# First attention of an attention and gMLP stack on one NeuronCore: no moves on ScalarE, output weights and four residual pairs loaded in the opening, pattern work on GpSimd in pieces, ring copies later

## The chip, the cores and the metric

One core of a Trainium2 chip. The time is that of one execution on the device, in microseconds (us); lower is better. Engines: TensorE (PE: matmuls; PEld: its weight loads), VectorE (DVE), ScalarE (ACT), GpSimd (POOL) and SyncE (SP). DMAs are issued by SP, ScalarE or GpSimd and run on 16 DMA engines.

## The reference

Four layers, attention, gMLP, attention, gMLP, each with a layernorm before it and a residual sum after it, on x of 2048 rows by 576 columns in bfloat16:

```
qkv = layernorm(x) @ wqkv                 # 32 heads of 18
k, v gathered at positions s, s-2, ..., s-14   # window 8, dilation 2, masked below 0
o = softmax(q k / sqrt(18)) v
x = x + o @ wo
z = gelu(layernorm(x) @ w_in); z1, z2 = halves of z
x = x + (z1 * (w_sp @ layernorm(z2) + b_sp)) @ w_out
```

The change concerns the first attention only.

## The kernel before

The order of the work in an attention layer is written by hand: inside `layer_A` every engine runs its instructions in program order (a manual schedule, L377). Even positions of the sequence stand before odd ones, so the dilated window becomes a contiguous one, and the sequence is cut into 17 query tiles (one of 128, then 120 each) with a halo of eight keys.

**Opening** (L602 to L736). SP loads x in groups, then the weights of v and of q and k, then the rest of x; one small load is ScalarE's. `build_window_rows` (L115) makes, from a few integers, the pattern that is added to the logits as 14 extra rows per head, so that positions outside the window vanish in the softmax: `part0` on VectorE and GpSimd, `part1` and `part2` on GpSimd, `part3` six transposes on TensorE and a copy by ScalarE into `win_pat`. 46 matmuls of the identity run meanwhile. Then each tile of x goes through statistics (`S_`, VectorE), the power -1/2 of the variance (`R_`, GpSimd, L646), the layernorm (`A_`, VectorE, L653) and a transpose into `xnT`: tiles 0 to 3 on TensorE (`T_pe`), tiles 4 to 15 by a DMA transpose that SP issues (`T_`, L263). The layernorm's output lies in four buffers `xn_bufs` in turn, so tile 12 waits until the transpose of tile 8 has landed, and tile 15 for that of tile 11.

`PG(d, qk, cc)` (L416) projects one group of 128 q or k columns (groups 0 to 4; group 4 holds 64) for 512 rows: five matmuls (L435), then an eviction by ScalarE or VectorE into a staging buffer `stg` (or a part of `win2a`, lent). When q and k of 1024 rows are there, up to eight heads are moved by DMAs from staging into `QK` (L457), each to its own 32 partitions. A list of engines, taken in turn, issues these moves; in the opening GpSimd, SP and ScalarE. The 40 moves of the first half are SP's 13, GpSimd's 20 and ScalarE's 7. `VW(t, hh)` (L405) projects v of a query tile into `v_ext`.

**Steps.** After the opening come four query tiles of v, six projections (L833; the first two of them need tiles 8 to 11 of `xnT`), and the logits of half a query tile, `L_mm(0)` (L472); then a loop of 34 steps, two per query tile. Step s issues the logits of s + 1, their exponential (ScalarE, L481), the product with v (`PV`, L495), VectorE's division (L501, L503), and what a table holds for that step: remaining projections in steps 0 to 11, v from step 12 on, and the output projection `WO` (L556) from step 13 on, with its residual sum (L559), store and next layernorm (GpSimd, L256). The logits of a tile need the moves of its heads: those of the first half of the heads groups 0 to 2, the others groups 2 to 4; from query tile 8 on they need the second half of the sequence too.

`PV` leaves o in one of four `o_bufs`. SP transposes it by DMA into the ring `oT` (L510), or, where the tile does not start at a multiple of 16, into one of two `o_slot` (L514), and VectorE copies it from there into the ring later (`O_CP`, L523). The step of that copy is `min(2t + 6, s)` for tile t, where s is the step before the output projection that needs it (L790): step 10 for tile 2, 14 for tile 4, 18 for tile 6, 22 for tile 8. `XO` (L541) loads the residual rows of two tiles: those of tiles 0 to 11 in steps 0 to 2. `load_wo` loads the output weights in step 4 (L824).

**Queues and waits.** The DMAs that SP and ScalarE issue share eight completion semaphores in turn, in program order; those of GpSimd have eight others. An issue waits until the DMA that had its semaphore before has landed, so that eight are in flight at most, and an engine that waits so does nothing else. SP issues transposes, moves and loads from one list, in order. PSUM holds a ring of tiles that TensorE fills in turn; a tile that is not evicted holds TensorE up.

Of the kernel before, what the change touches and what calls it, by code (L numbers as in the profile page):

```python
# [10 lines left out]
ALU = mybir.AluOpType  # L11
# [7 lines left out]
P = 128  # L19
# [44 lines left out]
class K:  # L64
# [50 lines left out]
    def build_window_rows(self, c, Wb):  # L115
# [38 lines left out]
            for xb in self.xn_bufs:  # L154
                e.memset(xb[:, D:640], 0.0)

        def part2():
            e = nc.gpsimd
            par = vf[:, 4, 3:4]
            e.tensor_scalar(out=hh[:, 1, :], in0=hh[:, 0, :], scalar1=0.0, scalar2=WB, op0=ALU.is_ge, op1=ALU.mult)  # L160
            e.tensor_scalar(out=W[:, 0, :, 0:8], in0=hh[:, 1:2, :].to_broadcast([P, 12, 8]), scalar1=-half, scalar2=par,
                            op0=ALU.add, op1=ALU.mult)
            e.tensor_scalar(out=hh[:, 2, :], in0=hh[:, 0, :], scalar1=-2.0, scalar2=-1.0, op0=ALU.is_equal, op1=ALU.mult)
            e.tensor_scalar(out=hh[:, 3, :], in0=hh[:, 0, :], scalar1=14.0, scalar2=None, op0=ALU.is_equal)
            e.tensor_tensor(out=hh[:, 2, :], in0=hh[:, 2, :], in1=hh[:, 3, :], op=ALU.add)
# [4 lines left out]
            e.tensor_tensor(out=uu[:], in0=vf[:, 0:4, 0], in1=vf[:, 0:4, 1], op=ALU.add)  # L170
            e.tensor_scalar(out=W[:, 1, :, 8:12], in0=uu[:, None, :].to_broadcast([P, 12, 4]), scalar1=0.5, scalar2=None,
                            op0=ALU.mult)
            e.memset(W[:, 1, 8:12, 8:9], 0.0)
            e.memset(W[:, 1, 8:12, 9:12], 1.0)
            e.memset(W[:, 0, 8:12, 11:12], 1.5 * WB)
            e.memset(W[:, 0, 8:12, 13:14], -3.5 * WB)

        def part3():
            pt = self.PT_tile([P, 6, P], bf16, "pt")
            for k_ in range(6):  # L180
                nc.tensor.transpose(pt[:, k_, :], Wb[:, k_ // 3, k_ % 3].rearrange("p j q -> p (j q)"), self.ident[:])
            nc.scalar.copy(out=pat[:], in_=pt[:].rearrange("p (a b) x -> p a (b x)", a=2)[:, :, 0:2 * P + 8])
        return part0, part1, part2, part3

    def make_ident(self):
        nc = self.nc
# [108 lines left out]
        nc, R = self.nc, self.right  # L295
        nc.vector.memset(R["wv"][64:128, 4, :], 0.0)

    def zero_more(self, eng):
        eng.memset(self.right["wqk4"][64:128, :], 0.0)
        eng.memset(self.right["wo"][64:128, 4, :], 0.0)  # L300

    def load_wqk(self, eng):
# [35 lines left out]
    def layer_A(self, li):  # L338
# [263 lines left out]
        if li == 0:  # L602
# [26 lines left out]
                nc.tensor.matmul(warm[:, 0:P], lhsT=self.ident[:], rhs=self.ident[:], start=True, stop=True)  # L629
            rows[2]()  # L630
            nc.scalar.copy(out=v_ext[:, :, :, DH:DH + 1], in_=self.ones[:, None, None, :].to_broadcast([P, NT, H, 1]))
            rows[3]()
            mvs = sb.tile([P, NS, 2], f32, name="lnx_mv", tag="lnx_mv", bufs=1)
            rstds = sb.tile([P, NS], f32, name="lnx_rstd", tag="lnx_rstd", bufs=1)

# [12 lines left out]

            def A_(*tiles):
                for i in tiles:  # L650
                    xns[i] = xn = self.xn_bufs[self.xn_rr % len(self.xn_bufs)]
                    self.xn_rr += 1
                    nc.vector.tensor_scalar(out=xn[:, 0:D], in0=xts[i], scalar1=mvs[:, i, 0:1],  # L653
                                            scalar2=rstds[:, i:i + 1], op0=ALU.subtract, op1=ALU.mult)

# [42 lines left out]
            A_(3)  # L698
            T_pe(3)
# [87 lines left out]
        for t in range(NT - 2):  # L787
            s = wo_steps[q0_(t) // P][0] - 1
            r = (q0_(t) + tdim(t)[1] - 1) // P - RING
            if t < NT - 3 and not in_ring(t):  # L790
                ocps.append((min(2 * t + 6, s), t))
                assert r < 0 or wo_steps[r][1] < min(2 * t + 6, s)
# [72 lines left out]
    def layer_B(self, li):  # L865
# [286 lines left out]
        for i in range(i0, NS):  # L1152
# [3 lines left out]
            p3_finish(i, acc)  # L1156
            if next_is_A and i == 2:
                self.zero_right()
                self.zero_more(nc.vector)
            if i >= 3 and late_loads:  # L1160
                late_loads.pop(0)()
        if (NS - 2) in xns:
# [72 lines left out]
```

## Time and profile before

| | us |
|---|---|
| median of 3 runs | 1175.58 |
| lowest, highest | 1175.12, 1177.72 |
| the profiled execution | 1177.02 |
| its span in the profile | 1175.2 |
| TensorE busy | 1150.6 |
| VectorE, ScalarE, GpSimd busy | 551.2, 341.8, 271.1 |
| first attention ends, gMLP begins (first L924 matmul) | 135.32 |

The profile is of one execution. A row of the timeline gives start, length, engine, line, operation, output and inputs, shape, count (x), and in brackets how long the engine had been idle and what ended it. `SPq`, `ACTq` are issues of DMAs by these engines; an issue is over long before its DMA has landed. A row of waits gives who waited, for whom, us in total, times, and the longest. The granted clock is the share of TensorE's full speed that it was given. Busy time of TensorE is not the same as speed: at half the clock it is busy and slow.

### The profile page before, as it was taken

Reading aid. Unit: us, or ns where it says so; the run is one execution under the profiler, and the core shown is the slowest. Engines: PE = TensorE matmul, PEld = TensorE weight load, DVE = VectorE, ACT = ScalarE, POOL = GpSimd, SP = SyncE. Lnnn points to the kernel's source line nnn. Section 1 sums busy time; section 2 is a strip of 40 time slices with the busy share of each in tenths; the row PEclk is TensorE's granted clock in tenths of the full one; section 3 lists DMA queues with packets and bytes.
Section 4 is the critical chain, followed back from the end, with each engine's and each line's share of the span. In section 5 each row is a group of like instructions: output and inputs, shape, how many; then the busy total and the mean of one; then the engine's idle time right before and its main releaser. Section 6 shows DMA issues by size and latency. Waiting matters only on the chain.

```text
span 1175.2 us, 19942 instructions
## 1 busy us (share of the span) xinstructions
PE 1150.6 (98%) x8169; PEld 611.8 (52%) x8264; DVE 551.2 (47%) x1166; ACT 341.8 (29%) x500; POOL 271.1 (23%) x389
## 2 busy tenths in 40 slices
PE   8889999999999999999999999999999999999998
PEld 5447644444444444447755675444444444444677
DVE  8468888422332332334465787863323223322321
ACT  5478655211101111101147884550011110111000
POOL 4468865100000000001144686540000000000000
PEclk9899999999999999999999999999999999999999
DMA  7799889000000000049646898950000000001332
GB/s 194 124 181 226 220 187 196 23 12 12 1 12 12 12 12 1 1 139 282 172 106 109 178 284 216 196 107 1 12 12 12 12 11 2 12 1 45 110 106 73
DMA packets 183242, 106.37 MB, mean 91 GB/s; under 512 B 135165, under 2 KB 164453, under 8 KB 183151
## 3 DMA queue, kind: packets, MB, share of 16 engines
q1 hardware_dynamic: 170140, 84.66, 31.4%
q0 software_dynamic: 6384, 14.28, 4.6%
q10 hardware_dynamic: 6627, 6.17, 1.8%
q8 instruction: 64, 1.05, 0.4%
q14 instruction: 27, 0.22, 0.1%
HBM read 42.34 MB, written 21.76 MB: 55 GB/s over the span
## 4 chain that ended last, share of the span: by engine, by line
PE 93%; DMA 2%; DVE 2%; POOL 1%; issue 1%; ACT 1%; ACTq 0%; DVEq 0%; POOLq 0%; SPq 0%
PE pg L1072 42%; PE po L1121 12%; PE pz L924 6%; PE pz L1048 6%; PE pz1s L1048 6%; PE pzs L924 6%; PE pp L435 6%; PE pw L556 3%; PE pv L409 3%; PE O_ps L495 2%; PE L_ps L472 1%; DMA o_slot<-o_t 1%; DMA QK<-stg 1%; POOL ln_xn L256 1%; ACTq L78 0%
## 5 line engine op out<-in xcount | busy, mean ns | idle before, releaser
L1072 PE MATMUL pg<-Wq,Z 128*128 128x512 bf16 x2260 | 497.9, 379 | 2.5
L1072 PEld LDWEIGHTS <-Z 128*128 128x128 bf16 x2304 | 225.4, 98 | 271.9
L1076 DVE TENSOR_TENSOR g_tmp<-pg,ln_xn 128x512 f32<-128x512 f32 x144 | 99.6, 692 | 421.6 <-PE pg L1072 419.5
L1067 ACT ACTIVATE z1T<-pz 128x1024 bf16<-128x1024 f32 x36 | 34.9, 1021 | 500.2 <-PE pz L1048 500.2
L78 POOL DMA_DIRECT2D wout<-in_B_w_out_dram x4 | 4.3, 1072 | 598.8 <-PE pg L1072 598.8
L1121 PE MATMUL po<-wout,Z 128*128 128x288 bf16 x1152 | 141.4, 286 | 0.0
L481 ACT ACTIVATE P_sb<-L_ps 128x1440 bf16<-128x1440 f32 (+3 forms) x136 | 125.1, 972 | 25.4 <-PE L_ps L472 23.7
L1121 PEld LDWEIGHTS <-Z 128*128 128x128 bf16 x1152 | 112.7, 98 | 28.8
L924 PEld LDWEIGHTS <-xnT 128*128 128x128 bf16 (+1 forms) x800 | 68.3, 97 | 75.8 <-issue 10.4
L1077 DVE TENSOR_TENSOR Z<-g_tmp,z1T 128x512 bf16<-128x512 f32 x144 | 99.7, 692 | 12.2
L973 DVE BATCH_NORM_STATS2 z_st<-zp 128x6 f32<-128x512 bf16 (+1 forms) x160 | 91.2, 617 | 9.1 <-ACT zp L971 8.9
L1048 PEld LDWEIGHTS <-w 128*128 128x128 bf16 (+1 forms) x640 | 53.8, 97 | 74.0 <-issue 13.6
L435 PE MATMUL pp<-xnT,wqk_sb 128*128 128x512 bf16 x341 | 82.3, 382 | 1.3 <-issue 0.2
L1131 DVE TENSOR_TENSOR x_new<-po,xo 128x288 f32<-128x288 f32 (+1 forms) x64 | 28.8, 456 | 87.8 <-PE po L1121 83.9
L1048 PE MATMUL pz<-xnT,w 128*128 128x512 bf16 (+1 forms) x316 | 66.3, 380 | 0.2
L1048 PE MATMUL pz1s<-xnT,w 128*128 128x512 bf16 (+1 forms) x310 | 64.9, 379 | 0.9 <-issue 0.8
L256 POOL TENSOR_SCALAR ln_xn<-x_new,ln_mv,ln_rstd 128x576 bf16<-128x576 f32 x28 | 64.1, 2290 | 3.2 <-DMA xn_rows<-ln_xn 0.6
L409 PE MATMUL pv<-wv_sb,xnT 128*128 128x288 bf16 x340 | 51.9, 294 | 9.6 <-ACT v_ext L403 5.0
L924 PE MATMUL pz<-win2a,xnT 128*128 128x512 bf16 (+1 forms) x233 | 58.3, 357 | 0.9 <-DVE x_new L559 0.5
L924 PE MATMUL pzs<-win2a,xnT 128*128 128x512 bf16 (+1 forms) x235 | 58.6, 358 | 0.4 <-issue 0.3
L997 POOL TENSOR_SCALAR Z<-zp,z_mv,z_rstd 128x256 bf16<-128x256 bf16 x32 | 54.5, 1703 | 3.4
L971 ACT ACTIVATE zp<-pz 128x1024 bf16<-128x1024 f32 (+2 forms) x56 | 36.6, 720 | 63.3 <-PE pz L924 63.3
(123 smaller groups left out, 936.2 us busy)
## 6 DMA issues: line engine op xcount, KB each, us to landing
xres<-x_new SPq DMA_DIRECT2D x48, 288.0 KB
xo<-xres SPq DMA_DIRECT2D x32, 288.0 KB
wout<-in_B_w_out_dram POOLq DMA_DIRECT2D x4, 1296.0 KB, 7.9
xn_rows<-ln_xn SPq DMA_DIRECT2D x32, 160.0 KB
w<-in_B_w_in_dram SPq DMA_DIRECT2D x16, 256.0 KB
QK<-stg POOLq DMA_DIRECT2D x50, 72.0 KB, 4.5
xo<-xres SPq DMA_DIRECT2D x6, 576.0 KB
QK<-stg SPq DMA_DIRECT2D x35, 72.0 KB
```

What stands on the lines that cost most here:

```text
L256: e.tensor_scalar(out=xn[:nrows, 0:D], in0=x_t[:nrows, :], scalar1=mv[:nrows, 0:1], scalar2=rstd[:nrows, 0:1], op0=ALU.subtract, op1=ALU.mult)
L409: nc.tensor.matmul(pv[:nk, 0:288], lhsT=self.xnT[:, c, k0_(t):k0_(t) + nk], rhs=wv_sb[:, c, hh * 288:(hh + 1) * 288], start=(c == 0), stop ...
L435: nc.tensor.matmul(pp[:, :], lhsT=w, rhs=self.xnT[:, c, cc * 512:(cc + 1) * 512], start=(c == 0), stop=(c == 4))
L481: nc.scalar.activation(out=P_bufs[2 * jp + s % 2][:nk, :, :, 0:nq], in_=Lv[:nk, :, :, 0:nq], func=ACT.Exp, scale=scale)
L924: nc.tensor.matmul(out[:, o0:o0 + n], lhsT=self.xnT[r0:r1, c, r * P:(r + 1) * P], rhs=win2(c)[r0:r1, w0:w0 + n], start=start, stop=stop, t ...
L973: nc.vector.bn_stats(out=st[:, x // 512, :], in_=zp[:, x:x + min(512, w0 + n - x)])
L997: eng.tensor_scalar(out=Z[:, b0:b1, i, :], in0=zv[:, b0:b1, :], scalar1=mv[:, 0:1], scalar2=rstd[:, 0:1], op0=ALU.subtract, op1=ALU.mult)
L1048: nc.tensor.matmul(outs[a_], lhsT=w1[r0:r1, c, sub * P:(sub + 1) * P], rhs=self.xnT[r0:r1, c, q * 512:(q + 1) * 512], start=start, stop=st ...
L1072: nc.tensor.matmul(pg[:, :], lhsT=Z[:, jj, i, sub * P:(sub + 1) * P], rhs=Wq[q][:, i, :], start=(i == 0), stop=(i == NS - 1))
L1076: nc.vector.tensor_tensor(out=tmp[:], in0=pg[:, :], in1=bsp[:, qs], op=ALU.add)
L1077: nc.vector.tensor_tensor(out=uT(jj)[:, sub, qs], in0=tmp[:], in1=z1Ts[jj, sub][:, qs], op=ALU.mult)
L1121: nc.tensor.matmul(acc[hh], lhsT=u_rows(j, i), rhs=wouts[j // NJH][:, j % NJH, hh * 288:(hh + 1) * 288], start=(j == 0), stop=(j == NJ - 1))
```

## The change

- `part2` (13 operations of GpSimd) becomes `part2a` (four), `part2b`, `part2c` and `part2d`. The first still stands ahead of the power of tile 0; the others stand behind the powers of tiles 0, 1 and 2.
- The six transposes of `part3` go behind the v projection `VW(1, 1)`, and the copy, now `part4`, behind `VW(2, 0)`.
- `zero_more` becomes `zero_wqk4` and `zero_wo`; the second, and the fills of `setup_bufs`, come later on GpSimd.
- The layernorms of tiles 12 to 14 are written into `o_bufs[1]` to `[3]` instead of `xn_bufs`. Tile 15 still uses `xn_bufs`, and waits for the transpose of tile 8.
- Moves in the opening: groups 0 and 4 by GpSimd and SP in turn, groups 1 to 3 by GpSimd, SP, GpSimd. Of the 40, SP issues 16, GpSimd 24, ScalarE none.
- `load_wo` and `XO` of tiles 0 to 7 (four loads of two tiles) are issued by SP in the opening, right behind the transposes of tiles 6 and 7, instead of in steps 4, 0 and 1. `XO` of tiles 8 and 9, and of 10 and 11, goes from step 2 to steps 19 and 22.
- The ring copies of `O_CP` stand at `min(2t + 8, s)`: step 12 for tile 2, 16 for tile 4, 19 for tile 6, 23 for tile 8; the others, and all those of the second attention, stay where they were.

```diff
-        def part2():
+        def part2a():
             e.tensor_scalar(out=hh[:, 1, :], in0=hh[:, 0, :], scalar1=0.0, scalar2=WB, op0=ALU.is_ge, op1=ALU.mult)
+            e.tensor_scalar(out=hh[:, 2, :], in0=hh[:, 0, :], scalar1=-2.0, scalar2=-1.0, op0=ALU.is_equal, op1=ALU.mult)
+            e.tensor_scalar(out=hh[:, 3, :], in0=hh[:, 0, :], scalar1=14.0, scalar2=None, op0=ALU.is_equal)
+            e.tensor_tensor(out=uu[:], in0=vf[:, 0:4, 0], in1=vf[:, 0:4, 1], op=ALU.add)
+        def part2b():
...
+        def part4():
+            nc.scalar.copy(out=pat[:], in_=pts[0][:].rearrange("p (a b) x -> p a (b x)", a=2)[:, :, 0:2 * P + 8])
...
-            rows[3]()
...
             def A_(*tiles):
                 for i in tiles:
-                    xns[i] = xn = self.xn_bufs[self.xn_rr % len(self.xn_bufs)]
-                    self.xn_rr += 1
+                    if 12 <= i < 15:
+                        xn = o_bufs[i - 11][:]
+                    else:
+                        xn = self.xn_bufs[self.xn_rr % len(self.xn_bufs)]
+                        self.xn_rr += 1
+                    xns[i] = xn
...
             S_(0)
             R_(0, 1)
             S1(1)
+            rows[3]()
             A_(0)
             S2(1)
             R_(1, 1)
+            rows[4]()
             T_pe(0)
...
             S2(2)
             R_(2, 1)
+            rows[5]()
             VW(1, 0, False)
             S_(3)
             A_(2)
             R_(3, 1)
-            self.zero_more(nc.gpsimd)
-            setup_bufs(nc.gpsimd)
+            self.zero_wqk4(nc.gpsimd)
             T_pe(2)
             VW(1, 1, False)
+            rows[6]()
...
             R_(4, 2)
+            self.zero_wo(nc.gpsimd)
+            setup_bufs(nc.gpsimd)
             VW(2, 0, False)
+            rows[7]()
             VW(2, 1, False)
...
             T_(6, 7)
+            self.load_wo(nc.sync)
+            for i in range(0, 8, 2):
+                XO(i)
...
-                    PG(d, qk, cc, False, (nc.gpsimd, nc.sync, nc.gpsimd, nc.scalar, nc.gpsimd, nc.sync))
+                    PG(d, qk, cc, False, (nc.gpsimd, nc.sync) if d in (0, 4) else q2)
...
-                ocps.append((min(2 * t + 6, s), t))
+                ocps.append((min(2 * t + 8, s), t))
...
-                at(max([i // 4 if li == 0 and i < 12 else s - 7] + [wo_steps[j][1] + 1 for j in last]), XO, i)
+                if li > 0 or i >= 8:
+                    at(max([s - 7] + [wo_steps[j][1] + 1 for j in last]), XO, i)
...
-            at(4, self.load_wo, nc.sync)
```

`q2` is GpSimd, SP, GpSimd (L599).

More of the change, by code (lines that the diff above doesn't have):

```diff
@@ L155, in part1, with part2c @@
                 e.memset(xb[:, D:640], 0.0)
-        def part2():
-            e = nc.gpsimd
-            par = vf[:, 4, 3:4]
+        e = nc.gpsimd
+        par = vf[:, 4, 3:4]
+        def part2a():
             e.tensor_scalar(out=hh[:, 1, :], in0=hh[:, 0, :], scalar1=0.0, scalar2=WB, op0=ALU.is_ge, op1=ALU.mult)
+            e.tensor_scalar(out=hh[:, 2, :], in0=hh[:, 0, :], scalar1=-2.0, scalar2=-1.0, op0=ALU.is_equal, op1=ALU.mult)
+            e.tensor_scalar(out=hh[:, 3, :], in0=hh[:, 0, :], scalar1=14.0, scalar2=None, op0=ALU.is_equal)
+            e.tensor_tensor(out=uu[:], in0=vf[:, 0:4, 0], in1=vf[:, 0:4, 1], op=ALU.add)
+        def part2b():
+            e.tensor_tensor(out=hh[:, 2, :], in0=hh[:, 2, :], in1=hh[:, 3, :], op=ALU.add)
             e.tensor_scalar(out=W[:, 0, :, 0:8], in0=hh[:, 1:2, :].to_broadcast([P, 12, 8]), scalar1=-half, scalar2=par,
                             op0=ALU.add, op1=ALU.mult)
-            e.tensor_scalar(out=hh[:, 2, :], in0=hh[:, 0, :], scalar1=-2.0, scalar2=-1.0, op0=ALU.is_equal, op1=ALU.mult)
-            e.tensor_scalar(out=hh[:, 3, :], in0=hh[:, 0, :], scalar1=14.0, scalar2=None, op0=ALU.is_equal)
-            e.tensor_tensor(out=hh[:, 2, :], in0=hh[:, 2, :], in1=hh[:, 3, :], op=ALU.add)
+        def part2c():
             e.tensor_scalar(out=W[:, 1, :, 0:8], in0=hh[:, 2:3, :].to_broadcast([P, 12, 8]), scalar1=par, scalar2=None,
@@ L169, in part2, with part2d @@
                             op0=ALU.mult)
-            e.tensor_tensor(out=uu[:], in0=vf[:, 0:4, 0], in1=vf[:, 0:4, 1], op=ALU.add)
+        def part2d():
             e.tensor_scalar(out=W[:, 1, :, 8:12], in0=uu[:, None, :].to_broadcast([P, 12, 4]), scalar1=0.5, scalar2=None,
                             op0=ALU.mult)
+            e.memset(W[:, 0, 8:12, 11:12], 1.5 * WB)
+            e.memset(W[:, 0, 8:12, 13:14], -3.5 * WB)
             e.memset(W[:, 1, 8:12, 8:9], 0.0)
             e.memset(W[:, 1, 8:12, 9:12], 1.0)
-            e.memset(W[:, 0, 8:12, 11:12], 1.5 * WB)
-            e.memset(W[:, 0, 8:12, 13:14], -3.5 * WB)
+        pts = []
         def part3():
@@ L181, in part3 @@
                 nc.tensor.transpose(pt[:, k_, :], Wb[:, k_ // 3, k_ % 3].rearrange("p j q -> p (j q)"), self.ident[:])
-            nc.scalar.copy(out=pat[:], in_=pt[:].rearrange("p (a b) x -> p a (b x)", a=2)[:, :, 0:2 * P + 8])
-        return part0, part1, part2, part3
+            pts.append(pt)
+        def part4():
+            nc.scalar.copy(out=pat[:], in_=pts[0][:].rearrange("p (a b) x -> p a (b x)", a=2)[:, :, 0:2 * P + 8])
+        return part0, part1, part2a, part2b, part2c, part2d, part3, part4
     def make_ident(self):
@@ L296, in zero_right, with zero_wqk4, zero_wo @@
         nc.vector.memset(R["wv"][64:128, 4, :], 0.0)
-    def zero_more(self, eng):
+    def zero_wqk4(self, eng):
         eng.memset(self.right["wqk4"][64:128, :], 0.0)
+    def zero_wo(self, eng):
         eng.memset(self.right["wo"][64:128, 4, :], 0.0)
@@ L790, in layer_A @@
             if t < NT - 3 and not in_ring(t):
-                ocps.append((min(2 * t + 6, s), t))
-                assert r < 0 or wo_steps[r][1] < min(2 * t + 6, s)
+                ocps.append((min(2 * t + 8, s), t))
+                assert r < 0 or wo_steps[r][1] < min(2 * t + 8, s)
             else:
@@ L1158, in layer_B @@
                 self.zero_right()
-                self.zero_more(nc.vector)
+                self.zero_wqk4(nc.vector)
+                self.zero_wo(nc.vector)
             if i >= 3 and late_loads:
```

## The prediction

> **What bounds the kernel now.** I read the page first, then busy time by stretches of the first attention, then its waits, then the timeline around the two longest. In the stretches the columns are length, busy time of TensorE, its loads, VectorE, ScalarE and GpSimd, then granted clock, DMA share and GB/s.
>
> ```profile
> span 1175.2 us, 19942 instructions
> PE 1150.6 (98%) x8169; PEld 611.8 (52%) x8264; DVE 551.2 (47%) x1166; ACT 341.8 (29%) x500; POOL 271.1 (23%) x389
> ...
> 35.00:40.00 5.00, 3.45 (x27) 2.54 (x26) 0.98 (x4) 1.07 (x2) 3.86 (x7) 1.00 1.07 99
> 40.00:45.00 5.00, 1.57 (x7) 0.99 (x7) 0.90 (x2) 1.78 (x6) 2.48 (x5) 0.75 1.17 153
> 45.00:50.00 5.00, 4.78 (x18) 2.35 (x17) 1.01 (x2) 1.03 (x3) 0.14 (x1) 0.57 0.63 123
> ...
> 80.00:85.00 5.00, 0.47 (x13) 0.33 (x10) 1.19 (x4) 1.73 (x2) 2.15 (x4) 0.84 1.22 137
> 85.00:90.00 5.00, 5.00 (x63) 2.88 (x61) 2.92 (x8) 1.83 (x2) 3.06 (x6) 0.50 0.98 148
> ```
>
> TensorE is the bound of the whole, so only its holes and its slow clock are worth anything. In the first attention there are two holes, near 40 and 82 us, and after each the granted clock is about half.
>
> ```profile
> PE pv L409 <- ACT v_ext L403: 5.0, 1, 5.0
> PE pv L409 <- DVE o_t L503: 4.5, 1, 4.5
> ACT v_ext L403 <- DMA QK<-win2a: 6.1, 1, 6.1
> DVE oT L523 <- DMA o_slot<-o_t: 5.5, 1, 5.5
> ```
>
> Behind each hole stands an engine that waits for a DMA: ScalarE in the first, VectorE in the second.
>
> ```profile
> 35.23 3.23 PE L409 MATMUL pv<-wv_sb,xnT 128*128 128x288 bf16 x25
> ...
> 41.33 1.61 ACTq L78 DMA_DIRECT2D QK<-win2a  x2
> 42.98 1.61 ACT L403 CAST v_ext<-pv 128x288 bf16<-128x288 f32 x5 [6.10 <-DMA QK<-win2a]
> ...
> 45.79 0.43 DVE L653 TENSOR_SCALAR ln_xn<-x_in,lnx_mv,lnx_rstd 128x576 bf16<-128x576 bf16 x1 [1.03 <-DMA xnT<-ln_xn]
> ...
> 50.38 0.40 PE L472 MATMUL L_ps<-QK 32*128 32x128 bf16 x16
> ...
> 56.36 0.40 PE L472 MATMUL L_ps<-QK 32*128 32x128 bf16 x16
> ```
>
> First hole: TensorE ends 25 value matmuls at 38.46 and waits for ScalarE's evictions, which stand behind two moves that ScalarE issues only at 41.33. But the next projections need xnT tile 11, and the 45.79 row shows when its transpose had landed (the layernorm there reuses that buffer). So with ScalarE free, this transpose is what is late next, and most of the hole stays.
>
> ```profile
> 74.55 1.84 SPq L514 DMA_TRANSPOSE o_slot<-o_t  x1
> ...
> 79.41 0.39 PE L472 MATMUL L_ps<-QK 32*128 32x120 bf16 x16
> 79.79 2.61 SPq L78 DMA_DIRECT2D QK<-stg  x3
> ...
> 83.78 0.35 DVE L523 COPY oT<-o_slot 128x600 bf16<-128x600 bf16 x1 [5.48 <-DMA o_slot<-o_t]
> ...
> 91.87 0.39 PE L472 MATMUL L_ps<-QK 32*128 32x120 bf16 x16
> ...
> 93.93 0.39 PE L472 MATMUL L_ps<-QK 32*128 32x120 bf16 x16
> ```
>
> Second hole: the ring copy of tile 2 (step 10) holds VectorE until its transpose lands. SP issued that transpose only at 74.55, and it landed 9.2 us later. The logits of steps 13 and 16 start 12.46 us apart, where three undisturbed steps (93.93 - 91.87 = 2.06 each) take 6.2.
>
> **The change, part by part.**
>
> *Opening.*
>
> ```profile
> 3.33 0.25 POOL L160 TENSOR_SCALAR win_hh<-win_hh 128x8 f32<-128x8 f32 x1 [0.72 <-DVE win_hh L145]
> ...
> 4.82 0.81 DVE L670 BATCH_NORM_STATS2 ln_st<-x_in 128x6 f32<-128x288 bf16 x2
> 6.74 0.58 POOL L646 TENSOR_TENSOR lnx_rstd<-lnx_rstd,neg_half 128x1 f32<-128x1 f32 x1
> 6.86 0.40 PE L181 MATMUL pt<-ident,oT 128*128 128x128 bf16 x4 [0.58 <-POOL oT L176]
> 7.29 0.60 ACT L182 COPY win_pat<-pt 128x528 bf16<-128x528 bf16 x1 [2.18 <-PE pt L181]
> 7.36 0.43 DVE L653 TENSOR_SCALAR ln_xn<-x_in,lnx_mv,lnx_rstd 128x576 bf16<-128x576 bf16 x1 [1.72 <-POOL lnx_rstd L646]
> ...
> 11.70 1.02 DVE L653 TENSOR_SCALAR ln_xn<-x_in,lnx_mv,lnx_rstd 128x576 bf16<-128x576 bf16 x1
> ...
> 14.29 8.80 PE L435 MATMUL pp<-xnT,wqk_sb 128*128 128x512 bf16 x39
> ```
>
> The first power stands behind all 13 pattern operations (3.33 to 6.74, 0.26 each). With four ahead of it, it ends by 5.6; the layernorm then waits only for the statistics that end at 5.63: 1.7 us earlier. Six transposes (0.40 for four, so 0.6) move from where TensorE waited into where it works. Net -1.1 at the first projection (14.29). The copy of 0.60 lies on ScalarE beside projections that leave it idle about half the time. Bounds: 0 (the nine other operations now beside VectorE's layernorms, each as slow as the 1.02 that stood beside a GpSimd fill) and -1.7.
>
> *No moves on ScalarE, weights and four pairs early.* Seven of 40 moves leave ScalarE: four go to GpSimd, three to SP. All six residual pairs and the output weights leave steps 0 to 4: two pairs go to steps 19 and 22; four pairs (295 KB each) and the weights (664 KB), 1.84 MB, go to SP after the transposes of tiles 4 to 7.
>
> ```profile
> DMA packets 2499, 2.10 MB, mean 300 GB/s; under 512 B 697, under 2 KB 2498, under 8 KB 2498
> ...
> DMA packets 22, 0.00 MB, mean 1 GB/s; under 512 B 22, under 2 KB 22, under 8 KB 22
> ...
> L78 POOL DMA_DIRECT2D QK<-stg x28: 526/587/663, 27.7 to 79.2; - x28
> ...
> DMA to landing us min/median/max: 1.6/6.1/9.3
> ...
> POOL QK L78 <- DMA QK<-stg: 8.3, 8, 1.5
> ```
>
> These are the DMA totals of 8 to 15 us (loads at 300 GB/s) and of 23.6 to 28.8 (idle), then the moves. At that rate the loads take 6.1 us, and 5.2 idle ones lie there: I take them as hidden, with 0 to +6.1 as bounds for what stands behind them on SP (four moves, then the transposes of tiles 8 to 11).
>
> First hole: the remaining 15 value matmuls (0.129 each from the x25 row) end at 38.46 + 1.9 - 1.1 = 39.3. Tile 11 lands at 45.79 - 1.1, and I take 1.0 off, since three of ScalarE's seven moves now stand behind the transposes on SP instead of beside them: 43.7. The trace bounds this loosely: nothing off, or as early as 40 if they landed alone.
>
> ```profile
> 48.40:49.40 1.00, 1.00 (x4) 0.31 (x3) 0.00 (x0) 0.00 (x0) 0.00 (x0) 0.56 0.60 133
> 49.40:50.40 1.00, 1.00 (x9) 0.32 (x11) 0.69 (x1) 0.00 (x0) 0.00 (x0) 1.00 0.57 104
> ```
>
> After a hole of 5.0 us the clock was half until 49.3 (a mean of 0.56 is 0.88 us of half), 5.8 us from the restart at 38.46 + 5.0. A hole from 39.3 to 44.0 will do the same. Ten projection matmuls (8.80/39 = 0.226, doubled) then take 4.5, and the first logits start at 48.5 instead of 50.38, with 1.3 us of slow clock left after them (0.6 lost): -1.3 for opening and first hole together. The page "TensorE: Matmul & The Clock Gate" of the Trainium skill (Part 1: The HAM clock gate) has the clock fall after one idle window of about 3.4 us and return after as long of work. The fall agrees with this trace, the 5.8 us do not; by its 3.4 the first hole would come out 1.2 us better.
>
> Whether taking ScalarE's queue away hurries tile 11 is the soft point. The page "DMA: Bandwidth & Descriptors" of the Trainium skill (Issuing engines are not separate DMA queues) says that all issuers' DMAs run on the same 16 engines and interleave, so that another issuer saves issue time only. No run yet shows which holds; by it my 1.0 falls away and the sum is 1.0 worse.
>
> *Second hole.*
>
> ```profile
> 60.72 0.98 SPq L78 DMA_DIRECT2D xo<-in_A_x_dram  x2
> ...
> 73.03 1.40 SPq L78 DMA_DIRECT2D wo_sb<-in_A_wo_dram  x2
> ```
>
> These are the first and last of four rows (eight issues, 0.98 + 1.11 + 1.57 + 1.40 = 5.06 us) that SP loses between 60 and 75, when it issues without a break; 2.4 MB leave with them, 8 us of DMA at 300 GB/s. The transpose of tile 2 is then issued some 5 us earlier against its steps, and its copy comes two steps later (step 12, 3.8 us). Either alone nearly covers the 5.48. So the hole goes: -(12.46 - 6.2) = -6.3. Late next are the moves of group 2 in the second half of the sequence, at 79.79 on SP now: at about 79.79 - 1.3 - 5 = 73.5 to 76 then, with 6.1 to land at 82, and the longest 9.3 at 85. The logits that need them (91.87 now) start at 84.3. Bounds of this part: -6.6 and, where those moves come last, -1.
>
> *Later copies of tiles 4, 6 and 8, layernorm of tiles 12 to 14 into attention buffers, fills in two parts:* nothing. Each copy still precedes the output projection by a step; the layernorms no longer wait for transposes, on an idle VectorE; the fills lie in GpSimd's idle time. If that cover is gone, a late copy costs one step, 2.06.
>
> **Sum.** -1.3 - 6.3 = -7.6. The profiled execution took 1177.02 (span 1175.2 and 1.8 around it) and becomes 1169.4; it lies 1.4 above the median of the three runs, 1175.58, which becomes 1168.0. I forecast 1168.0, by itself 1166 to 1170.5.
>
> **Rivals.** *Early transposes* (0.18): tile 11 lands by 40 and the clock never falls. Then the last moves bound the second logits (56.36 now): with eight in flight at 6.1, GpSimd's 24 go out every 0.76 us from 26.6 (27.7 - 1.1) to 44.9 and land by 51; with the longest landing time for the last one, 54. At 52 it is -4.4 instead of -1.3: 1165. For it: one issuing queue fewer, and transposes that took 8 us to land in a crowd. Against: GpSimd's queue is fuller, and it is the crowd.
>
> *The loads collide* (0.10): the whole 6.1 goes before tile 11; the first logits come at 54.6, +4.7, and with -6.3 the time is 1174. Against: the idle 5.2 us.
>
> *The second hole moves* (0.12): the logits at 84.3 wait for moves that land at 88, and lose 2.9 to the clock after it; about -0.9 remains: 1174.5; half of the cases stop at 1172.
>
> *Slower* (0.10): GpSimd's moves. It has 24 instead of 20, each 0.587 to issue, with eight in flight, and already waits eight times for a landing. If each takes the longest 9.3, one goes out per 1.16 us: the last at 26.6 + 27.9 = 54.5, landing at 63.8. The second logits need it at 55.1: +8.7, +2.9 of slow clock (half of 5.8), -7.6 from the sum: 1179.6. It decides once that last move lands after 55; the median of 6.1 speaks against it.
>
> **Chances.** Forecast 0.50, the rivals 0.18, 0.10, 0.12, 0.10. A measurement of this kernel tells about 0.2% (2.4 us) from no change. Faster: 0.50 + 0.18 + half of each of the two middle rivals, 0.78 rounded; within: their other halves, 0.12; slower: 0.10. The range, 1163.5 to 1175, leaves out the slower case and the tails.
>
> **What would show it.** Right: no ScalarE moves; the first projection near 13.2; the first logits near 48.5, after a shorter hole that ends with tile 11; no wait of VectorE for the tile 2 transpose; steps 12 to 16 at 2.06 each with full clock; the second layer and everything after unchanged in length. Wrong: a layernorm or projection waiting for a DMA beyond 45, GpSimd still issuing first-half moves at 50, or TensorE waiting at the logits of step 16.

## The result, and the profile after

| | before | after |
|---|---|---|
| median of 6 runs, us | 1175.60 | 1168.38 |
| lowest, highest | 1175.00, 1177.72 | 1167.56, 1169.42 |
| the profiled execution | 1177.02 | 1168.93 |
| its span | 1175.2 | 1167.2 |
| first projection of the opening | 14.29 | 12.63 |
| first logits | 50.38 | 47.18 |
| logits of step 13, of step 16 | 79.41, 91.87 | 76.22, 82.25 |
| first gMLP matmul | 135.32 | 126.26 |

The ratio of the times is 0.9935, 95% interval 0.9923 to 0.9948. In the two profiled executions the first gMLP matmul comes 9.06 us earlier: 3.20 at the first logits, 6.43 between steps 13 and 16 (6.03 instead of 12.46), and 0.56 lost between step 16 and the gMLP. From there to the end of the span it is 1167.2 - 126.26 = 1040.94 us, and was 1039.88: 1.06 us go again. The profiled execution of before lies 1.4 us above its median, so all landmarks below that are set against it show a little more than the medians. (The logits of step n are those of the n-th half query tile, counted from 0; the loop issues them in its step n - 1.)

The same stretches of the first attention after the change (columns as in the prediction's view):

```profile
35.00:40.00 5.00, 3.97 (x33) 2.94 (x30) 1.45 (x4) 2.93 (x8) 4.70 (x8) 1.00 1.35 147
40.00:45.00 5.00, 1.40 (x3) 0.59 (x5) 0.00 (x0) 0.00 (x0) 2.67 (x5) 0.81 0.82 119
45.00:50.00 5.00, 5.00 (x35) 2.12 (x34) 3.33 (x4) 2.28 (x3) 0.03 (x1) 0.84 0.68 143
80.00:85.00 5.00, 5.00 (x118) 3.64 (x116) 4.69 (x17) 4.55 (x7) 3.69 (x7) 1.00 0.93 153
```

The last stretch is full and at full clock: the second hole is gone. The first is not. From 40 to 45 us VectorE and ScalarE have no work at all, and ScalarE's last eviction of a value tile ends at 39.40, so it does not hold TensorE up any more. The timeline of TensorE there:

```profile
33.90 5.06 PE L423 MATMUL pv<-wv_sb,xnT 128*128 128x288 bf16 x40
43.38 0.59 PE L449 MATMUL pp<-xnT,wqk_sb 128*128 128x512 bf16 x1 [4.41 <-DMA QK<-win2a]
...
47.18 0.40 PE L486 MATMUL L_ps<-QK 32*128 32x128 bf16 x16
```

All 40 value matmuls now run in one piece and end at 38.96; then the projections wait 4.41 us. The releaser named is a move, but a projection reads xnT, not QK. In kernels 2 and 8 below the same row names `xnT<-ln_xn`: it is the transpose of tile 11.

The second hole's place, in the timelines of SP, VectorE and TensorE:

```profile
66.73 1.25 SPq L528 DMA_TRANSPOSE o_slot<-o_t  x1
...
76.22 0.39 PE L486 MATMUL L_ps<-QK 32*128 32x120 bf16 x16
78.14 0.39 PE L486 MATMUL L_ps<-QK 32*128 32x120 bf16 x16 [0.40 <-ACT P_sb L495]
78.18 0.34 DVE L537 COPY oT<-o_slot 128x600 bf16<-128x600 bf16 x1
80.19 0.39 PE L486 MATMUL L_ps<-QK 32*128 32x120 bf16 x16
82.25 0.39 PE L486 MATMUL L_ps<-QK 32*128 32x120 bf16 x16
...
87.57 0.65 DVE L537 COPY oT<-o_slot 128x600 bf16<-128x600 bf16 x1
88.28 0.79 PE L570 MATMUL pw<-wo_sb,oT 128*128 128x288 bf16 x5 [0.40 <-DVE oT L537]
```

SP issues tile 2's transpose at 66.73 instead of 74.55, and the copy at 78.18 has no wait in brackets. The last two rows are the new small loss: the copy of tile 4, now two steps later, ends after the output projection wants it. The step of these rows, step 18 by the count of the logits (86.36 to 88.99; the expectations below call it 17), takes 2.63 us instead of 2.06, and 2.31 in the second profile of the same kernel (kernel 9).

### The profile page after: what moved, and what is told of

Same layout as the page of the kernel before. It is cut to its first block, busy times and chain, and to the rows that moved or that the text cites. A ratio compares the mean times of both kernels' runs of the same rounds, so it can differ in the third digit from the quotient of the medians.

```text
span 1167.2 us, 19947 instructions
## 1 busy us (share of the span) xinstructions
PE 1147.4 (98%) x8169; PEld 610.4 (52%) x8264; DVE 551.2 (47%) x1166; ACT 342.4 (29%) x500; POOL 273.8 (23%) x393
## 3 DMA queue, kind: packets, MB, share of 16 engines
q8 instruction: 64, 1.05, 0.4%
## 4 chain that ended last, share of the span: by engine, by line
PE 96%; DVE 1%; issue 1%; ACT 1%; DMA 0%; SPq 0%; DVEq 0%; ACTq 0%
PE pg L1098 42%; PE po L1147 12%; PE pp L449 7%; PE pz L950 6%; PE pz L1074 6%; PE pz1s L1074 6%; PE pzs L950 6%; PE pv L423 3%; PE pw L570 3%; PE O_ps L509 2%; PE L_ps L486 2%; ACT P_sb L495 1%; DVE ln_st L581 0%; DVE x_new L573 0%; DMA xres<-x_new 0%
## 5 line engine op out<-in xcount | busy, mean ns | idle before, releaser
L78 POOL DMA_DIRECT2D QK<-stg x76 | 46.5, 615 | 40.7 <-DVE stg L415 23.7
L449 PEld LDWEIGHTS <-wqk_sb 128*128 128x128 bf16 x360 | 33.4, 98 | 42.3 <-DMA QK<-win2a 4.7
```

What stands on the lines that cost most here:

```text
L78: return eng.dma_start(out=out, in_=in_)
L449: nc.tensor.matmul(pp[:, :], lhsT=w, rhs=self.xnT[:, c, cc * 512:(cc + 1) * 512], start=(c == 0), stop=(c == 4))
```

## The experiments

The kernels were measured in three groups, each beside runs of the kernel before on the same chip: 1 to 4 (median of before 1174.58), 6, 7, 8 and 10 (1174.48), and 5, 9, 11 and 12 (1175.0). Ratios are against those. Kernels 1 to 4 put one part of the change into the kernel before (the buffers of the layernorms of tiles 12 to 14 were not tried alone); 5 to 8 take one part out of the changed kernel, or move it within; 9 is the changed kernel again; 10 to 12 carry the theory further.

**1. The pattern part alone (e1_pieces).**

```diff
-            rows[3]()
...
             R_(0, 1)
             S1(1)
+            rows[3]()
             A_(0)
             S2(1)
             R_(1, 1)
+            rows[4]()
```

> The kernel before with the pattern work alone changed (GpSimd pieces, transposes and fills later; moves, loads, layernorm buffers and copies as before). Theory: the first projection starts at 12.6 us as in the changed kernel (14.29 before), all that follows in the opening comes 1.5 earlier with it, tile 11's transpose too, so the first logits come at 48.9 instead of 50.38; the second hole stays; total 1.5 us below before, ratio 0.9987. Rival: the first hole, which ends with a DMA's landing, swallows the opening's gain: first logits at 50.4, total unchanged.

1172.47 us, ratio 0.9981 [0.9966, 0.9995]. First projection at 12.63, first logits at 47.10. ScalarE is still stuck behind its moves, and VectorE behind tile 2's transpose; two waits around the two holes:

```profile
PE pv L423 <- ACT v_ext L417: 4.1, 1, 4.1
DVE oT L537 <- DMA o_slot<-o_t: 4.3, 1, 4.3
```

The opening's 1.66 us are real, and the second hole (steps 13 to 16 in 11.41) stays. The first logits come 3.28 us earlier, twice what the theory gave: in this trace TensorE's idle time in the first hole is also shorter, 4.10 instead of 4.98.

**2. The moves' queues alone (e2_queues).**

```diff
-                    PG(d, qk, cc, False, (nc.gpsimd, nc.sync, nc.gpsimd, nc.scalar, nc.gpsimd, nc.sync))
+                    PG(d, qk, cc, False, (nc.gpsimd, nc.sync) if d in (0, 4) else q2)
```

> The kernel before with the moves of the opening on GpSimd and SP only, nothing else changed. Theory (tile 11's transpose sets the end of the first hole, and ScalarE's queue only competes with it a little): the 40 value matmuls run through without a stop, the hole then lasts until tile 11 has landed at 44 to 45, first logits at 49 to 49.5 instead of 50.38, total 1 us below before. Rival A (ScalarE's stuck issue sets the hole): first logits at 47.2 or earlier, total 3 us below. Rival B (GpSimd's longer list of moves comes last): second logits later than 56.4, total above before.

1175.3 us, ratio 0.9997 [0.9984, 1.0011]: no difference. Yet the first logits come at 45.73, 4.65 earlier. The timeline of the first hole, then a wait from the second:

```profile
35.39 5.06 PE L409 MATMUL pv<-wv_sb,xnT 128*128 128x288 bf16 x40
43.48 2.32 PE L435 MATMUL pp<-xnT,wqk_sb 128*128 128x512 bf16 x10 [3.02 <-DMA xnT<-ln_xn]
```

```profile
DVE oT L523 <- DMA o_slot<-o_t: 7.2, 1, 7.2
```

The value matmuls run through, TensorE waits 3.02 us for the transpose, and the ten projections take 2.32: full clock. The theory had the wait right, but not the time: tile 11 lands at 43.4 instead of 44 to 45 and the clock stays full, so the first logits come earlier than even rival A had them. Steps 13 to 16 then take 13.55 us instead of 12.46, so 1.09 of the 4.65 us are waited out at the transpose of tile 2, which TensorE's speed does not hasten; 2.94 are left at the first gMLP matmul (132.38), 1.6 at the end of the span (1173.6), and none between the medians, since the profiled execution of before lay above its median.

**3. The early loads alone (e3_loads).**

```diff
+            self.load_wo(nc.sync)
+            for i in range(0, 8, 2):
+                XO(i)
...
-            at(4, self.load_wo, nc.sync)
```

> The kernel before with the output weights and four residual pairs loaded in the opening (and the last two pairs in steps 19 and 22), nothing else changed. Theory (SP's full list makes the transpose of tile 2 late, and the loads find an idle stretch of the DMA engines): that transpose is issued 5 us earlier, VectorE's copy in step 10 waits under 1 us instead of 5.5, clock full through steps 12 to 16, which take 6.2 instead of 12.5; first logits within 0.5 of 50.38; total 6 us below before. Rival A (the loads collide with moves and transposes): first logits later by 2 to 6 us, total within 2 us of before. Rival B (the copy's step matters, not the loads): VectorE still waits 3 us or more, total 2 us below.

1171.61 us, ratio 0.9974 [0.9960, 0.9988]. First logits at 48.78. The copy of tile 2 stands in step 10 as before, and has no wait left:

```profile
68.39 1.26 SPq L514 DMA_TRANSPOSE o_slot<-o_t  x1
...
76.62 0.34 DVE L523 COPY oT<-o_slot 128x600 bf16<-128x600 bf16 x1
77.82 0.39 PE L472 MATMUL L_ps<-QK 32*128 32x120 bf16 x16
...
83.85 0.47 PE L472 MATMUL L_ps<-QK 32*128 32x120 bf16 x16
```

Steps 13 to 16 take 6.03 us. The loads alone close the second hole. Tile 11 lands no later for them: the layernorm that waits for it starts at 45.01, and at 45.79 before. The time is 3.0 us below before where the theory gave 6: of the 8.0 that this trace has gained at the logits of step 16, 0.85 are lost up to the gMLP and 1.97 behind it, and before's profile lies 2.4 above the median of this group.

**4. The later copies alone (e4_copies).**

```diff
-                ocps.append((min(2 * t + 6, s), t))
+                ocps.append((min(2 * t + 8, s), t))
```

> The kernel before with the ring copies two steps later at most (steps 12, 16, 19, 23), nothing else changed. Theory: the transpose of tile 2 still lands near 83.8, the copy in step 12 (about 82) waits 1.9 instead of 5.5, TensorE's hole is too short for the clock to fall, and steps 12 to 16 take 8 us instead of 12.5: total 4.4 us below before. Rival: the lateness is SP's and moves along with the copy (the next transposes are as late): hole and slow clock stay, total within 1 us of before.

1174.8 us, ratio 0.9995 [0.9981, 1.0009]: no difference.

```profile
82.75 0.46 DVE L503 TENSOR_TENSOR o_t<-O_ps,rec 128x288 bf16<-128x288 f32 x1 [3.22 <-DMA o_slot<-o_t]
83.31 2.56 PE L556 MATMUL pw<-wo_sb,oT 128*128 128x288 bf16 x10 [2.16 <-DVE o_t L503]
85.80 0.59 PE L472 MATMUL L_ps<-QK 32*128 32x120 bf16 x16
89.04 0.39 PE L472 MATMUL L_ps<-QK 32*128 32x120 bf16 x16
```

VectorE still waits for the same transpose, only elsewhere: the division of tile 6 wants the `o_t` buffer of tile 2 (there are four), which the transpose is still reading. Steps 13 to 16 (78.35 to 89.04) take 10.69.

**5. The change with its loads back in the steps (f2_loads_steps).**

```diff
-            self.load_wo(nc.sync)
-            for i in range(0, 8, 2):
-                XO(i)
...
+            at(4, self.load_wo, nc.sync)
```

> The changed kernel with the output weights and all six residual pairs issued by SyncE in steps 0 to 4 again, as before the change; opening, queues, pieces and later copies as changed. Theory (the loads alone close the second hole, the later copies do not): the hole is back, steps 13 to 16 take 9 to 13 us instead of 6.0, with VectorE waiting 3 us or more for a transposed o_slot; first logits 45 to 47; 1171.5 to 1174 us. Rival (the prediction's step, either alone nearly covers it): steps 13 to 16 in 6 to 7.5 us, 1168 to 1169.5 us.

1173.62 us, ratio 0.9987 [0.9968, 1.0006]. The hole is back, with the later copies in place:

```profile
81.53 0.46 DVE L517 TENSOR_TENSOR o_t<-O_ps,rec 128x288 bf16<-128x288 f32 x1 [5.54 <-DMA o_slot<-o_t]
82.09 2.56 PE L570 MATMUL pw<-wo_sb,oT 128*128 128x288 bf16 x10 [4.48 <-DMA QK<-stg]
84.58 0.59 PE L486 MATMUL L_ps<-QK 32*128 32x120 bf16 x16
87.39 0.39 PE L486 MATMUL L_ps<-QK 32*128 32x120 bf16 x16
```

Steps 13 to 16 (74.81 to 87.39) take 12.58, much as in the kernel before. (The second row names a move; its matmuls start just after the division, as in kernel 4, where the same row names `o_t`.)

**6. The change with its copies back at 2t + 6 (f1_copies6).** The diff of kernel 4, the other way.

> The changed kernel with the ring copies back at step 2t+6, all else as changed. Theory (moving the loads off SyncE closed the second hole alone; the transpose of tile 2 is issued at 66.7, and lands before step 10 begins near 70 or soon after): no wait of VectorE for a DMA over 1.5 us, steps 13 to 16 in 6.0 to 6.6, and step 17, where a projection waited for a late copy, 2.06 instead of 2.63: 1167.9 us, from 0.5 faster to 0.5 slower than the changed kernel. Rival (the delay is needed too): the hole comes back in part, VectorE waits 2 us or more for a transpose, 1170 to 1172 us.

1167.4 us, ratio 0.9941 [0.9924, 0.9959]. No copy waits, steps 13 to 16 take 6.03, and step 18 takes 2.05 (85.15 to 87.20) instead of 2.63. The delay is not needed once the loads are out of SP's way. The first projection of this trace starts at 13.71, though the opening is that of the changed kernel: VectorE waits 1.63 us there for a load of x.

**7. The change with ScalarE issuing moves again (f3_act_moves).** The diff of kernel 2, the other way.

> The changed kernel with ScalarE again issuing its share (every sixth) of the moves. Theory (the landing of tile 11 sets the first logits, ScalarE's queue does not): ScalarE's evictions wait for a move again (4 us or more) and the value matmuls break in two parts, but the first logits come at 47 to 48 and the time is 1168 to 1169.5 us. Rival (ScalarE's moves did hold up the path, the queue part alone had gained 4.65 us there): first logits at 50 or later, 1171 us or more.

1170.12 us, ratio 0.9971 [0.9957, 0.9985].

```profile
34.49 3.23 PE L423 MATMUL pv<-wv_sb,xnT 128*128 128x288 bf16 x25
40.97 3.67 PE L423 MATMUL pv<-wv_sb,xnT 128*128 128x288 bf16 x15 [3.25 <-ACT v_ext L417]
44.44 2.36 PE L449 MATMUL pp<-xnT,wqk_sb 128*128 128x512 bf16 x10
46.73 0.40 PE L486 MATMUL L_ps<-QK 32*128 32x128 bf16 x16
```

ScalarE holds the value matmuls up again, but the first logits come at 46.73, no later than the 47.18 of the changed kernel's first profile: tile 11 has landed by the time the split value matmuls end. (In kernels 6 and 9, without ScalarE's moves, they come at 45.15 and 44.32; this trace also starts its projections late, at 13.84, after 1.77 us of waiting for a load of x.) The time lies 0.8 us above kernel 8 and 2.7 above kernel 6, both of the same group, and its interval overlaps both (that of 6 only just). It fits neither the theory nor the rival: a small cost is possible, not shown.

**8. The change with its loads behind the transposes of tiles 12 to 15 (f5_loads_late).**

```diff
             T_(6, 7)
-            self.load_wo(nc.sync)
-            for i in range(0, 8, 2):
-                XO(i)
```

(the three lines stand behind `T_` of tiles 12 to 15 instead)

> The changed kernel with the output weights and the four pairs issued by SyncE behind the transposes of tiles 12 to 15 instead of behind those of tiles 4 to 7. Theory (the loads in the opening do cost: they stand before the transposes of tiles 8 to 11 on SyncE and share the engines with the moves; that is why the first logits came only 3.2 us early, at 47.18, though the pattern part alone gave 3.28 and the queue part alone 4.65): tile 11 lands near 41.7 (43.37 of the queue part alone, less the 1.66 of the opening), first logits near 45, second near 51, the second hole stays closed (steps 13 to 16 in 6.2) since the weights have still left SyncE's queue by 50; 1166.3 us. Rival (the loads lie in the idle stretch and the moves set the landing): first logits 47.2, 1168.4 us. Second rival: the loads now collide with the last moves, second logits late by 2 to 6 us, 1170 to 1174.

1169.29 us, ratio 0.9959 [0.9946, 0.9971].

```profile
41.57 3.20 PE L449 MATMUL pp<-xnT,wqk_sb 128*128 128x512 bf16 x10 [3.21 <-DMA xnT<-ln_xn]
```

The trace looks like the theory (tile 11 by 41.57, first logits at 44.71), but the time is not the theory's 1166.3, and kernel 9 shows the same early landing with the loads in the opening.

**9. The changed kernel once more (a_again).**

> The changed kernel once more, so that the three beside it are compared with it on one chip and the scatter of its first hole is seen: 1167.5 to 1169.5 us, first logits between 45 and 48.5, according to how long the clock stays at half (not at all, 3.4 or 6.8 us).

1169.08 us, ratio 0.9949 [0.9925, 0.9972].

```profile
42.07 2.32 PE L449 MATMUL pp<-xnT,wqk_sb 128*128 128x512 bf16 x10 [2.75 <-issue]
44.32 0.40 PE L486 MATMUL L_ps<-QK 32*128 32x128 bf16 x14
```

The same program now has its first logits at 44.32, 2.86 us earlier than in its first profile, with the loads in the opening. The theory that they delay tile 11 falls; the difference is scatter of the transpose's landing (42.07 against 43.38) and of the clock. (Whether both profiles are of one chip is not on record.) Kernel 4 shows the same against before: up to step 10 it is the same program, and its first logits come at 49.31 instead of 50.38. That the loads are hidden shows in the DMA's columns, last but one the share of busy time, last GB/s, of the kernel before and then of after:

```profile
24.00:26.00 2.00, 1.82 (x10) 1.00 0.00 0
26.00:28.00 2.00, 2.00 (x11) 1.00 0.00 0
```

```profile
24.00:26.00 2.00, 2.00 (x11) 1.00 1.09 330
26.00:28.00 2.00, 2.00 (x11) 1.00 1.01 317
28.00:30.00 2.00, 2.00 (x11) 1.00 0.64 174
```

They fill the stretch that was idle, and the rate has fallen to 174 GB/s from 28 us on, where the moves run. The times agree: 1169.29 for kernel 8, with the loads late, and 1169.08 here.

**10. Early transposes (f4_early_transposes).** If tile 11's transpose among the moves is the first hole, issuing it ahead of them should remove it.

```diff
             T_(6, 7)
-            self.load_wo(nc.sync)
-            for i in range(0, 8, 2):
-                XO(i)
+            S_(9, 10, 11)
+            R_(8, 4)
+            A_(8, 9, 10, 11)
+            T_(8, 9, 10, 11)
```

(the loads as in kernel 8; tiles 9 to 11 instead of 12 to 14 are normalized into `o_bufs`)

> The changed kernel with statistics, layernorm and transposes of tiles 8 to 11 right behind those of tiles 6 and 7, before any move is issued, and the weights and four pairs behind the transposes of tiles 12 to 15. Theory (the first hole is tile 11's transpose among the moves): the transposes land by 37, the value matmuls run on into the projections without a hole, the clock does not fall, first logits at 42 to 43 (-4.5), second logits bound by the last moves at 49 to 52; 1164 us. Rival (the transposes take the place of the moves, whose landing then sets the first logits): a hole of the same size before the logits, which wait for a DMA of the windows; 1167 to 1169 us.

1164.28 us, ratio 0.9927 [0.9906, 0.9947].

```profile
33.29 5.06 PE L423 MATMUL pv<-wv_sb,xnT 128*128 128x288 bf16 x40
38.19 2.32 PE L449 MATMUL pp<-xnT,wqk_sb 128*128 128x512 bf16 x10
40.45 0.44 PE L486 MATMUL L_ps<-QK 32*128 32x128 bf16 x16
...
47.88 0.23 PE L486 MATMUL L_ps<-QK 32*128 32x128 bf16 x1 [0.71 <-DMA QK<-win2a]
```

No hole, no slow clock, first logits at 40.45 and first gMLP matmul at 120.61, 5.65 earlier than after. What waits now is one logits matmul of the second step, 0.71 us for a move. Kernel 8 of the same group, with the loads in the same place and the transposes among the moves, took 5.0 us more. That confirms the cause of the first hole. Two of the ten executions took 1172.0 and 1172.8, the others 1163.4 to 1165.9; what happened in the two was not profiled.

**11. Early transposes, copies back at 2t + 6 (g1_early_copies6).** Kernels 10 and 6 together.

> Early transposes of tiles 8 to 11 (first hole gone) with the ring copies back at step 2t+6. Theory (the delay of the copies bought nothing and costs a late copy in step 17): first logits 40.5, no second hole, 0.3 to 0.6 us faster than early transposes alone: 1163.8 us, 4 to 5 us faster than the changed kernel beside it. Rival (with the steps 7 us earlier, the transposes of tile 2 and 4 land too late for copies at 2t+6): VectorE waits 2 us or more for a DMA and a hole comes back, 1165 to 1168 us.

1163.7 us (1162.78 to 1165.56), ratio 0.9899 [0.9878, 0.9919]; the changed kernel beside it took 1169.08. This is the lowest median of all, 5.4 us below the change; that it is faster than kernel 10 is not shown (the two intervals overlap, and the first gMLP matmul comes at 120.77, against 120.61). In this trace the steps from 14 to 28 follow each other without a break, at 72.63 to 101.42, 2.06 each.

**12. Early transposes, loads ahead of the moves (g2_early_loads_open).**

```diff
             T_(8, 9, 10, 11)
+            self.load_wo(nc.sync)
+            for i in range(0, 8, 2):
+                XO(i)
```

(the loads no longer stand behind the transposes of tiles 12 to 15; the rest is kernel 10)

> Early transposes of tiles 8 to 11, with the weights and four pairs issued right behind them in the opening, ahead of SyncE's first moves, instead of behind tiles 12 to 15. Theory (the loads do cost the moves something where these set the pace): SyncE's moves go out 3.7 us later, some of the first logits' windows land late: first logits at 41 to 44 or second logits at 48 to 50 instead of 46.5; 1165 to 1167 us. Rival (the loads lie in the idle stretch and cost nothing anywhere): first and second logits at 40.5 and 46.5, 1164.3 us.

1173.4 us, ratio 0.9974 [0.9961, 0.9987]: 9.1 us above the median of kernel 10 and 9.7 above that of kernel 11, which is of the same group, and far more than the theory's 1165 to 1167. The rows of the stretch, then of GpSimd, VectorE and TensorE:

```profile
30.50:31.50 1.00, 1.00 (x7) 1.00 1.10 369
```

```profile
39.94 1.12 POOL L78 DMA_DIRECT2D QK<-stg  x2 [0.68 <-DMA QK<-stg]
41.08 1.04 POOL L659 TENSOR_TENSOR lnx_rstd<-lnx_rstd,neg_half 128x4 f32<-128x4 f32 x1
...
42.16 1.45 DVE L670 TENSOR_SCALAR ln_xn<-x_in,lnx_mv,lnx_rstd 128x576 bf16<-128x576 bf16 x4 [10.07 <-DMA QK<-stg]
43.52 1.28 DVE L415 CAST stg<-pp 128x512 bf16<-128x512 f32 x2
...
44.26 0.54 PE L486 MATMUL L_ps<-QK 32*128 32x128 bf16 x12 [3.23 <-DVE stg L415]
45.37 7.12 PE L449 MATMUL pp<-xnT,wqk_sb 128*128 128x512 bf16 x20
```

The same 1.84 MB now run beside the first moves. GpSimd waits for landings between its issues, so the power that stands behind them ends at 42.12 instead of 38.29 (37.25 + 1.04 in kernel 10); VectorE, in order, sits in the layernorm that needs it (the row names a move, but starts 0.04 us after the power ends); an eviction waits behind the layernorm, and twelve of the first logits' matmuls for the eviction. Then the clock halves (granted 0.50 from 44.40 to 50.40): 20 projections take 7.12 us, and 4.49 in kernel 10.

## Why the prediction was right, and where it was not

**Opening.** Forecast -1.1, measured -1.66 (12.63), at the edge of its bounds. Kernel 1 shows it alone. The first layernorm starts 1.77 us earlier (5.59 instead of 7.36), as forecast; the six transposes, 0.50 us at 10.58, cost next to nothing where 0.6 was put, because they fill a stretch in which TensorE had waited 0.35 us for a layernorm. Where a load of x comes late, less is left: 0.58 in kernel 6, 0.45 in kernel 7.

**Loads hidden.** Right, by the idle stretch that the prediction read from the profile of before (the rows under kernel 9). Kernel 12 shows what the same loads cost without that cover.

**Tile 11 sets the end of the first hole.** Right, and its time too: 43.7 forecast, 43.38 and 42.07 measured. The soft 1.0 us for ScalarE's queue stays unresolved. By the instruction that waits for it, and with the earlier opening added back, tile 11 lands at 43.7 to 45.8 where ScalarE issues moves (before, kernels 1, 3 and 4) and at 43.2 to 45.0 where it does not (2, 5, 6, 8 and both profiles of the change). The means differ by 1.1, the way that was forecast, but landings of one program scatter by as much, and these kernels differ in more than the queue. What ScalarE's moves did do is hold its own evictions (kernels 1, 3, 4 and 7).

**The slow clock after the hole.** The prediction said "A hole from 39.3 to 44.0 will do the same", that is 5.8 us of half clock, and so -1.3 for opening and first hole together. This term was mis-sized: -3.2 in one profile, -6.1 in the other. Of the 1.9 us by which the first profile does better, 0.6 are the earlier restart (43.38 instead of 44.0); the other 1.3 are the clock, half for 3.42 us instead of 5.8. Granted clock (the number after the bracket) at the start and end of the slow stretch, before, then after:

```profile
42.40:43.40 1.00, 0.00 (x0) 0.53 1.39 94
```

```profile
42.40:43.40 1.00, 0.02 (x1) 0.87 0.82 127
...
46.40:47.40 1.00, 1.00 (x20) 0.92 0.56 105
```

A mean of m in a window of 1 us is 2(1 - m) us of half clock. Before, that is 0.94 here, 5 whole rows, and 0.88 in the row at 48.40: 6.82. After: 0.26 + 3 rows + 0.16 = 3.42. Summed in this way, with the idle time of TensorE before it went on:

| kernel | idle, us | half clock, us | first logits |
|---|---|---|---|
| changed, copies at 2t+6 (6) | 2.71 | 0 | 45.15 |
| changed, second profile (9) | 2.75 | 0 | 44.32 |
| queues alone (2) | 3.02 | 0 | 45.73 |
| changed, loads late (8) | 3.21 | 3.40 | 44.71 |
| early transposes, loads ahead of the moves (12) | 3.23 | 6.82 | 40.80, most at 44.26 |
| changed, ScalarE moves (7) | 3.25 | 3.42 | 46.73 |
| changed, loads in steps (5) | 3.47 | 3.42 | 45.77 |
| loads alone (3) | 4.01 | 3.42 | 48.78 |
| pattern alone (1) | 4.10 | 6.82 | 47.10 |
| copies alone (4) | 4.14 | 6.82 | 49.31 |
| changed, first profile | 4.41 | 3.42 | 47.18 |
| before | 4.98 | 6.82 | 50.38 |

The slow stretch is none, one or two pieces of 3.4 us, and the 5.8 that the prediction read was the part of two pieces that lay behind the restart. The page "TensorE: Matmul & The Clock Gate" of the Trainium skill (Part 1: The HAM clock gate) has a free-running window of 3413 ns; the 3.40 to 3.42 here agree. The prediction gave that page's figure beside its own, and took its own from one hole, in which two windows stood one behind the other. How many pieces come does not follow from the idle time: 3.23 us gave two, 4.41 one. Nor is a whole piece of idleness needed ahead of the fall, as the prediction has it from that page: in kernel 1 the clock falls 2.0 us after TensorE went idle (at 38.6; idle from 36.6), and in kernel 8 an idle time of 3.21 was enough, with the fall 1.3 us behind its end (42.86; restart at 41.57).

**Second hole.** Forecast -6.3, measured -6.43, for half of the reason. "Either alone nearly covers the 5.48" failed: the loads alone do (kernel 3), the copies alone do not (kernel 4), and without the loads the hole stays whatever the copies do (kernel 5). Moving the copy moved the wait to the next user of the transpose, the reuse of `o_t`. With the loads gone SP issues the transpose 3.75 us ahead of the logits of step 10 (70.48), where it had issued it 0.88 behind them (73.67). These 4.6 us are most of the 5.48 that VectorE waited. The loads leave SP's list and the DMA engines of these steps together, though, and no kernel separates the two. Nothing was late behind the hole: the logits of step 16 ran without a wait at 82.25.

**Later copies: nothing.** "Each copy still precedes the output projection by a step" failed for tile 4: its copy ends after the projection wants it, which costs 0.57 us in step 18 (in the second profile that step is 0.25 longer than 2.06). Kernel 6 does not have this loss. That it shows in the time is not shown: kernel 11 has the copies back too, and its attention ends no earlier than that of kernel 10.

**Everything after unchanged.** 1.06 us longer in the first profile, 1.25 in the second (1165.3 - 124.17 = 1041.13 against 1039.88). With the copies alone it was 1039.91, but 1041.50, 1041.22 and 1041.85 with the pattern, the queues or the loads alone, so no single part explains it. The granted clock is full all through this part in both profiles. Most of the difference is one wait at the start of the second gMLP, where a matmul waits for a residual sum: 0.46 us before, 1.05 and 1.29 after. In the first profile VectorE waits 2.63 us instead of 2.03 ahead of that sum, for a DMA (`xres<-x_new`); why this DMA comes later was not settled.

The sum came out near because these errors cancel: the first hole gave more, step 18 and the part behind the attention took back 1.6. That closeness is luck: against the span of before the first profile is 8.0 us shorter, and the second, of the same kernel, 9.9. The two holes, and what ends the first, were read rightly. The four parts alone give -2.1, +0.7, -3.0 and +0.2 us by their medians, -4.1 together, and the whole -7.2. That may be noise (each of the four is known to about 1.6 us), or gains of one part that are waited out at the hole which another part closes, as kernel 2 has it.

## What to carry to other kernels

Before a late wait is moved, ask who else needs the same transfer: here, moving the consumer of a late DMA shifted the wait, and taking other loads off the issuing queue ahead of it removed it. Put the transfers that the next stage of TensorE needs ahead of a crowd of small ones, and large loads into a stretch in which the DMA is idle; issued 8 us later, beside the moves, they cost 9 us here (kernel 12). And take a second profile before reading a landing time that differs by 1 or 2 us as the effect of an edit.

## What the runs showed of the hardware

- TensorE's slow clock came in pieces of 3.4 us: idle times of 2.71 to 3.02 us cost none, of 3.21 to 4.98 one or two (the table above). The clock fell as early as 2.0 us into an idle time (kernel 1) and as late as 1.3 us behind its end (kernel 8). Beside the idle time itself, a piece costs up to half its length, 1.7 us (less where TensorE stands idle in part of it).
- Landing times of the same program scatter: tile 11's transpose by 1.3 us between two profiles, and, with the clock behind it, the first logits by 2.86.
- An engine that issues moves among its own work waits for landings there: the 15 moves that GpSimd issues ahead of the power took 8.55 us from the first issue in kernel 10, without a wait, and from 28.85 to 41.06 beside the loads in kernel 12.
